# A recurrent attention with a gated feed-forward: the state update moved into the chunk's product, and all chunks ordered anew

## The chip, the cores and the metric

The kernel runs on one core of a Trainium2 chip. The metric is the device time of one execution in microseconds (us), as the median of several runs. The engines are TensorE (PE in the rows; PEld is its loading of weights), VectorE (DVE), ScalarE (ACT), GpSimd (POOL) and SyncE (SP, which issues the DMAs).

## What is computed

```python
# q, k, v, alpha: (4, 8, 768, 48); w_in: (384, 2048); w_out: (2048, 384)
for t in range(S):
    state = alpha[:, :, t, :, None] * state + np.einsum('bhd,bhe->bhde', k[:, :, t], v[:, :, t])
    y[:, :, t] = np.einsum('bhd,bhde->bhe', q[:, :, t], state)
x = np.ascontiguousarray(attn_out.transpose(0, 2, 1, 3)).reshape(B * S, H * D)   # (3072, 384)
h = x @ w_in
sp = np.where(h > 20.0, h, np.log1p(np.exp(np.minimum(h, 20.0))))
return ((h * np.tanh(sp)) @ w_out).astype(np.float32)
```

## The kernel before

**Chunks.** The 768 steps of each of 4 batches are cut into 6 chunks of 128; the 24 chunks are numbered with the batch running fastest, so chunk n follows chunk n - 4 of the same batch. For each chunk `attention(n)` records these tasks. VectorE makes decays by two scans and multiplies keys and queries with them (L523 to L550). *Scores*: TensorE multiplies keys with queries into two PSUM banks (L570, 16 matmuls, which the trace shows as 32 records, two passes of float32 each). VectorE masks them into `probs` (L580). *Product*: into two further banks, three groups of 8 matmuls: state times queries (only from the second chunk of a batch on), values times the diagonal-free half of `probs` on 128 rows, values times the diagonal blocks on 64 rows (all L625; 16 records a group). A tiny memset on GpSimd between the first and the last group keeps matmuls of different row groups apart. ScalarE and VectorE split the product into a high and a low part (L641, L646; for the first 8 chunks TensorE subtracts, L653, and ScalarE copies, L661), and six small DMAs move rows together.

**State.** For all but the last chunk of a batch there are four steps more: *turn*, 4 transposes of the decayed keys on TensorE into a fifth bank (L732); a copy of them to SBUF on ScalarE (L736, one buffer, tag `kb`); *update*, 8 matmuls of keys with values into a sixth bank (L743); and *gather*, on VectorE, which adds that bank to the decayed state (L753; for the first chunk of a batch a copy on ScalarE, L751).

**Units.** A feed-forward unit takes 2 or 4 chunks and one of 16 slices of 128 hidden columns: 9 matmuls of "up" (L782), a chain of five ScalarE and three VectorE passes (L791 to L817), then three matmuls of "down" for each chunk (L845) into an accumulating bank `o0` to `o3`. There are 106 units.

**What sets the order.** Nothing is issued in the order of recording. `Plan.order` walks all tasks with a planner's cost and latency (table `COST`) and a due time (`key`, shifted by hand in the table `SHIFT`), picks at each step the task that can begin first, and thereby fixes the order of every engine's queue. Each queue runs in order on the chip. PSUM banks come from queues too: two called `att`, two `h`, and `o0` to `o3`; `EARLY_BANKS` lets some chunks use free `h` and `o` banks. Until planned time 130 the planner puts a *fill* matmul (L895, whose result nobody reads) wherever it sees TensorE with nothing to do. The framework adds the semaphores; two engines that touch one PSUM bank are kept apart by a semaphore, whatever columns they touch.

Of the kernel before, what the change touches and what calls it, by code (L numbers as in the profile page):

```python
# [27 lines left out]
B, H, S, D = 4, 8, 768, 48  # L28
DM, FF = 384, 2048
P = 128  # L30
C = 128
HALF = C // 2
NCH = S // C
NPAIR = H // 2
R = 112
# [32 lines left out]
    0: "h att o2 att o2 o0".split(),  # L68
    1: "att att att att h att".split(),
    2: "att o1 o1 o3 att att".split(),  # L70
    3: "att h o3 o1 att o0".split(),
    4: "att att att h att att".split(),
    5: "o3 att att o2 att att".split(),
    6: "att att att att h att".split(),
    7: "att att att att o2 o3".split(),
# [3 lines left out]
        4: -2, 5: -2, 7: 2.79, 21: -1,  # L79
    },  # L80
    "unit": {
# [3 lines left out]
    },  # L85
    "weight": {
        0: -5, 4: 5.7, 11: 4, 14: 2, 15: 1,
    },
    "weight check": {
        5: 15, 9: 5,  # L90
    },
}
X_PE = 8
W_PE = 3
# [16 lines left out]
class Task:  # L111
    def __init__(self, engine, cost, late, key, emit, port):
        self.engine, self.cost, self.late, self.key, self.emit = engine, cost, late, key, emit
        self.port = port
        self.needs, self.behind, self.uses, self.begin = [], [], [], None


class Plan:
# [14 lines left out]
    def add(self, engine, cost, late, key, emit, needs=(), uses=(), behind=(), port=False):  # L133
        t = Task(engine, cost, late, key, emit, port)
        t.needs, t.uses, t.behind = list(needs), list(uses), list(behind)
        for u in t.uses:
            u.left += 1
            u.key = min(u.key, key)
        self.tasks.append(t)
        return t  # L140

    def order(self):
# [9 lines left out]
        moving, landed = 0.0, []  # L152
# [40 lines left out]
        while len(done) < n + fills:  # L193
            best = None
            for e in ENGINES:
                first = None
                for t in waiting[e][:WINDOW]:
# [3 lines left out]
                    r = max(r, free[e], port_free if t.port else 0.0)  # L201
# [22 lines left out]
            free[e] = at + t.cost  # L224
            if e == "SP":
# [19 lines left out]
WINDOW = 150  # L245
QUEUE = 8
# [7 lines left out]
    "scan": (1.16, 1.27), "inverse": (0.09, 0.21), "mult": (0.6, 0.72), "half mult": (0.345, 0.46), "check": (0.2, 0.34),  # L254
    "state": (0.365, 0.4), "state0": (0.31, 0.35), "mask": (0.49, 0.63),
    "scores": (1.02, 1.05), "y0": (1.1, 1.2), "y": (1.77, 1.79), "turn": (0.42, 0.64),
    "turned": (0.43, 0.57), "update": (0.7, 0.9),
    "x hi": (0.275, 0.415), "x lo": (0.34, 0.455),
    "down": (0.531, 0.8), "stash": (0.4, 0.53), "join": (0.47, 0.59), "result": (0.5, 0.7),
}  # L260
for _n in range(1, 5):
    _c = 128 * _n
    COST["up", _n] = (9 * (0.4333e-3 * _c + 0.009), 9 * (0.4333e-3 * _c + 0.009) + 0.205)
    COST["exp", _n] = (0.22 + 0.836e-3 * _c, 0.29 + 0.836e-3 * _c)
# [7 lines left out]
def fast_path(ctx, tc, qka, v, w, out, good):  # L272
# [203 lines left out]
    def attention(n):  # L476
# [5 lines left out]
        banks = EARLY_BANKS.get(n, ["att"] * 6)  # L482
# [103 lines left out]
        def product():  # L586
            p = [by_slot(within(z)) for z in y_buf]
            ops = []

            def head(j, a, lead, l, r, t=slice(0, C)):  # L590
                m, side = j // 2, 1 ^ a ^ (j // 2)
                wide = D if side else HALF
                ops.append(
                    (
                        p[m][64 * side : 64 * side + wide, j % 2, t], l(wide), r,
                        j % 2 == 0 and lead,
                    )
                )

            if not first:  # L600
                for i in range(2):
                    for j in (i, i + 2):
                        for a, r in enumerate((0, 64)):
                            head(
                                j, a, True, lambda w: st[r : r + D, j * D : j * D + w],
                                Q()[r : r + D, j],
                            )
            for j in range(NPAIR):
                for a in (1, 0) if j < 2 else (0, 1):
# [4 lines left out]
                    )  # L614
            for i in range(2):
                for j in (i, i + 2):
                    rows = slice(HALF * (j // 2), HALF * (j // 2) + HALF)
                    for a in (1, 0) if j < 2 else (0, 1):
                        h = (2 * j + a) * D
                        head(  # L620
                            j, a, False, lambda w: V()[rows, h : h + w],
                            probs[slot[a]][rows, i, 0], slice(0, HALF),
                        )
            for m, (o, l, r, begins) in enumerate(ops):
                made = nc.tensor.matmul(  # L625
                    o, l, r, start=begins, stop=m >= len(ops) - 2, skip_group_check=True
                )
                if not first and m == 7:
                    apart = nc.gpsimd.memset(between, 0.0)
                    tc.add_manual_dep(apart.ins, made.ins.name, SYNCED, reason="rows apart")  # L630
                if not first and m == 16:
                    tc.add_manual_dep(made.ins, apart.ins.name, SYNCED, reason="rows apart")
# [56 lines left out]
        if not first:  # L689
# [6 lines left out]
        t_sc = add("PE", *COST["scores"], key + 0.2, scores, [*t_k, t_q], [q_buf, *sc_buf])  # L696
# [6 lines left out]
        ]  # L703
        t_y = add(
            "PE", *COST["y0" if first else "y"], key + 0.5, product,
            [*t_mask, t_q, got_v, *t_decay], [q_buf, v_buf, *y_buf],
# [20 lines left out]
        kb_buf, u_buf, ks_buf = bank(banks[4]), bank(banks[5]), plan.buffer("kb")  # L727

        def turn():
            p = by_pair(within(kb_buf))  # L730
            for j in range(NPAIR):
                nc.tensor.transpose(p[:, j, :R], K()[:, j], ident[:R, :R])  # L732

        def turned():
            t = new(ks_buf, [P, NPAIR, R], f"ks{n}")
            nc.scalar.copy(t, by_pair(kb_buf.tile)[:, :, :R])  # L736

        def update():
            p = by_pair(within(u_buf))
            for j in range(NPAIR):  # L740
                for a, wide in ((0, HALF), (1, D)):
# [427 lines left out]
```

## Time and profile before

| | us |
|---|---|
| three runs | 516.72, 517.62, 518.61 |
| median | 517.62 |
| the profiled execution's own time | 516.63 |
| its span in the trace | 514.9 |
| TensorE busy | 506.9 |
| ScalarE busy | 393.6 |
| VectorE busy | 377.4 |

The span lies 1.7 us below the execution's own time: what lies around it isn't traced. The records of matmuls overlap, since they are pipelined, so a group's own "us" in a timeline is longer than the time to the next group's start. The time that a group costs is read from start to next start.

### The profile page before, as it was taken

To read this page: it belongs to the slowest core of one execution; us is meant where nothing else is said; L and a number is where in the kernel's file an instruction comes from. 1 tells how busy PE (TensorE), PEld (TensorE's weight loads), DVE (VectorE), ACT (ScalarE), POOL (GpSimd) and SP (SyncE) were. 2 spreads that over 40 slices of the span, in tenths; PEclk is the share of its full clock that TensorE was granted. 3 is DMA by queue.
4 is the path that set the end of the run, shared out by engine and by line. 5 is a ranking of instruction groups with operands and counts; after the bars stand their busy time and mean duration, and the time that the engine had idled before them with its cause. 6 is when DMAs were issued, how large, how long until landed. Compare 5 with 4: busy or idle time off the path is not lost.

```text
span 514.9 us, 11417 instructions
## 1 busy us (share of the span) xinstructions
PE 506.9 (98%) x4448; PEld 439.7 (85%) x4448; DVE 377.4 (73%) x729; ACT 393.6 (76%) x908; POOL 4.6 (1%) x34
## 2 busy tenths in 40 slices
PE   7999999999999999999999999999999999999996
PEld 4688899898988888888889888889878899999996
DVE  8999999999987878677765567676479544444442
ACT  2587789988699989988977676668766767787774
POOL 2000000000000000000000000000000000000000
PEclk9999999999999999999999999999999999999999
DMA  7684425332336765356420042220032000010001
GB/s 275 232 281 160 149 92 201 122 123 64 122 125 209 238 238 206 125 208 210 147 84 0 1 148 86 87 84 1 16 133 86 9 9 0 23 40 1 0 2 65
DMA packets 20074, 56.68 MB, mean 110 GB/s; under 512 B 4016, under 2 KB 12464, under 8 KB 20016
## 3 DMA queue, kind: packets, MB, share of 16 engines
q1 hardware_dynamic: 20016, 55.91, 31.3%
q8 instruction: 36, 0.59, 0.4%
q14 instruction: 22, 0.18, 0.1%
HBM read 48.82 MB, written 4.72 MB: 104 GB/s over the span
## 4 chain that ended last, share of the span: by engine, by line
PE 94%; DVE 3%; DMA 1%; ACT 0%; issue 0%; DVEq 0%
PE bank L845 40%; PE bank L782 39%; PE bank L625 6%; PE bank L570 3%; PE bank L743 2%; PE bank L732 1%; PE bank L895 1%; DMA qka<-in_qka_dram 1%; DVE probs L580 1%; DVE rest L523 0%; DVE qka L540 0%; PE bank L653 0%; DVE w_lead L397 0%; PE bank L431 0%; DVE qka L550 0%
## 5 line engine op out<-in xcount | busy, mean ns | idle before, releaser
L845 PE MATMUL bank<-wo,g 128*128 128x384 f32 x1152 | 224.2, 341 | 0.0
L782 PE MATMUL bank<-xs,wi 128*128 128x512 f32 (+1 forms) x954 | 217.0, 374 | 0.0
L845 PEld LDWEIGHTS bank<-wo,g 128*128 128x128 f32 x1152 | 198.7, 188 | 7.1 <-ACT state L751 0.2
L782 PEld LDWEIGHTS bank<-xs,wi 128*128 128x128 f32 x954 | 166.6, 188 | 28.5 <-DVE y L801 0.2
L817 DVE TENSOR_TENSOR g<-t,g 128x512 fp32r<-128x512 f32 (+1 forms) x106 | 67.0, 636 | 50.3 <-ACT g L814 50.2
L801 DVE SCALAR_TENSOR_TENSOR y<-u,bank 128x512 f32<-128x512 f32 (+1 forms) x106 | 66.8, 631 | 42.0 <-ACT u L791 41.3
L791 ACT ACTIVATE u<-bank 128x512 f32<-128x512 f32 (+1 forms) x106 | 58.5, 552 | 45.0 <-PE bank L782 44.5
L814 ACT ACTIVATE g<-t 128x512 fp32r<-128x512 f32 (+1 forms) x106 | 61.3, 584 | 22.1 <-PE bank L845 16.1
L810 DVE SCALAR_TENSOR_TENSOR t<-y,t 128x512 f32<-128x512 f32 (+1 forms) x106 | 67.0, 632 | 14.8 <-ACT t L807 14.5
L804 ACT ACTIVATE t<-t,tenth 128x512 f32<-128x512 f32 (+1 forms) x106 | 72.1, 681 | 2.1
L797 ACT ACTIVATE t<-u 128x512 f32<-128x512 f32 (+1 forms) x106 | 62.5, 590 | 10.1 <-DVE g L817 8.6
L807 ACT ACTIVATE t<-t 128x512 f32<-128x512 f32 (+1 forms) x106 | 61.9, 584 | 0.7
L523 DVE TENSOR_TENSOR_SCAN rest<-qka,behind 112x516 f32<-112x516 f32 x24 | 29.4, 1226 | 4.6 <-DMA qka<-in_qka_dram 4.4
L540 DVE TENSOR_TENSOR_SCAN qka<-qka,ahead 112x516 f32<-112x516 f32 x24 | 29.3, 1223 | 0.0
L580 DVE COPY_PREDICATED probs<-causal,bank 128x384 f32<-128x384 uint32 x48 | 25.7, 583 | 2.5 <-PE bank L570 2.5
L625 PEld LDWEIGHTS bank<-probs,v 128*64 128x64 f32 (+3 forms) x768 | 20.7, 128 | 6.4 <-issue 3.3
L641 ACT ACTIVATE xs<-bank 112x256 fp32r<-112x256 f32 x48 | 16.1, 376 | 13.1 <-PE bank L625 12.8
L625 PE MATMUL bank<-probs,v 128*64 128x64 f32 (+3 forms) x768 | 25.6, 227 | 0.3
L570 PEld LDWEIGHTS bank<-qka 48*64 48x64 f32 x768 | 18.0, 133 | 6.5 <-issue 4.1
L570 PE MATMUL bank<-qka 48*64 48x64 f32 (+1 forms) x768 | 21.6, 250 | 0.4 <-issue 0.4
L791 ACT ACTIVATION_READ_ACCUMULATOR u<-bank 128x1 f32 x106 | 20.7, 195 | 0.0
L535 DVE TENSOR_TENSOR qka<-qka,rest 112x256 f32<-112x256 f32 x48 | 19.2, 401 | 0.0
(79 smaller groups left out, 321.2 us busy)
## 6 DMA issues: line engine op xcount, KB each, us to landing
qka<-in_qka_dram SPq DMA_DIRECT2D x22, 770.5 KB, 4.6
ws<-in_wp_dram SPq DMA_DIRECT2D x16, 768.0 KB, 4.3
wc<-in_wp_dram SPq DMA_DIRECT2D x16, 768.0 KB, 5.1
v<-in_vp_dram SPq DMA_DIRECT2D x24, 192.0 KB, 4.4
out_dram<-osb SPq DMA_DIRECT2D x16, 192.0 KB, 2.2
xs<-xs SPq DMA_DIRECT2D x144, 16.0 KB, 2.3
out_dram<-part SPq DMA_DIRECT2D x8, 192.0 KB, 2.8
qka<-in_qka_dram SPq DMA_DIRECT2D x2, 258.5 KB, 3.5
```

The lines of the kernel that those rows point to most:

```text
L570: nc.tensor.matmul(p[a][to, i, blocks], K()[r : r + D, j, to], q.rearrange("p (x t) -> p x t", t=HALF), start=True, stop=True,)
L625: made = nc.tensor.matmul(o, l, r, start=begins, stop=m >= len(ops) - 2, skip_group_check=True)
L782: nc.tensor.matmul(p[:, :N], wi[:, z, s, fs], x[:, s, :, a], start=m == 0, stop=m == len(passes) - 1,)
L791: nc.scalar.activation(wide(u), wide(h), AF.Exp, scale=-1.0, accum_out=uchk[:, at : at + 1])
L797: nc.scalar.activation(wide(t), wide(u), AF.Square, bias=1.0, scale=2.0)
L801: nc.vector.scalar_tensor_tensor(wide(y), wide(u), 0.5, wide(h), ALU.add, ALU.mult)
L804: nc.scalar.activation(wide(t), wide(t), AF.Ln, bias=tenth, scale=0.1)
L807: nc.scalar.activation(wide(t), wide(t), AF.Exp, scale=-1.0)
L810: nc.vector.scalar_tensor_tensor(wide(t), wide(y), 0.4, wide(t), ALU.mult, ALU.mult)
L814: nc.scalar.activation(g.tile[:, 0, :N], wide(t), AF.Copy)
L817: late[mybir.EngineType.DVE] = nc.vector.tensor_tensor(g.tile[:, 1, :N], wide(t), g.tile[:, 0, :N].bitcast(F32), ALU.subtract)
L845: made = nc.tensor.matmul(o.tile[:, :DM], g.tile[:, a, j * C : (j + 1) * C], wo[:, z, f], start=begins and m == 0, stop=end and m == 2,)
```

## The change

The 8 matmuls of the update are issued within the product: behind the second group (128 rows) and ahead of the third (64 rows). Their sums go to columns 256 to 447 of the product's first bank, which the product leaves free; the sixth bank is gone, and a chunk takes 5 banks. The turn and ScalarE's copy of the keys are now due right after the keys are decayed (0.15 and 0.2 behind the chunk's key instead of 0.8 and 0.85), and the product waits for that copy. The gather reads the product's first bank, which ScalarE (high part), and VectorE or TensorE (low part), read or write as well. The last chunk of a batch has no update, as before.

The planner takes 0.2 us off a task when two of scores and products follow each other on TensorE, many of its task times are new, and the tables `EARLY_BANKS` (19 chunks instead of 8) and `SHIFT` are new throughout, so all queues have a new order.

```diff
 SHIFT = {
     "chunk": {
-        4: -2, 5: -2, 7: 2.79, 21: -1,
+        5: -0.9, 6: -1.5, 7: -0.06, 10: 1, 11: 1, 12: -4, 13: -2, 14: -0.5, 15: 2.3, 17: -1,
...
-                    r = max(r, free[e], port_free if t.port else 0.0)
+                    saved = SAME if e == "PE" and small and t.small[0] else 0.0
+                    r = max(r, free[e] - saved, port_free if t.port else 0.0)
...
-        banks = EARLY_BANKS.get(n, ["att"] * 6)
+        banks = EARLY_BANKS.get(n, ["att"] * 5)
...
         def product():
             p = [by_slot(within(z)) for z in y_buf]
+            change = within(y_buf[0])[:, 2 * C : 2 * C + NPAIR * D].rearrange(
+                "p (j e) -> p j e", j=NPAIR
+            )
...
+            if not last:
+                for j in range(NPAIR):
+                    for a, wide in ((0, HALF), (1, D)):
+                        h = (2 * j + a) * D
+                        nc.tensor.matmul(
+                            change[64 * a : 64 * a + wide, j],
+                            ks_buf.tile[:, j, 64 * a : 64 * a + wide],
+                            V()[:, h : h + D], start=False, stop=True, skip_group_check=True,
+                        )
...
+            t_kb = add("PE", *COST["turn"], key + TURN_AT, turn, t_k, [q_buf, kb_buf])
+            t_ks = add("ACT", *COST["turned"], key + TURN_AT + 0.05, turned, [t_kb], [kb_buf, ks_buf])
         t_y = add(
-            "PE", *COST["y0" if first else "y"], key + 0.5, product,
-            [*t_mask, t_q, got_v, *t_decay], [q_buf, v_buf, *y_buf],
+            "PE", *COST["y0" if first else "y last" if last else "y"], key + 0.5, product,
+            [*t_mask, t_q, got_v, *t_decay] + ([] if last else [t_ks]),
+            [q_buf, v_buf, *y_buf] + ([] if last else [ks_buf]), small=(not first, True),
         )
...
-        kb_buf, u_buf, ks_buf = bank(banks[4]), bank(banks[5]), plan.buffer("kb")
...
-        def update():
-            p = by_pair(within(u_buf))
-            for j in range(NPAIR):
-                for a, wide in ((0, HALF), (1, D)):
-                    h = (2 * j + a) * D
-                    nc.tensor.matmul(
-                        p[64 * a : 64 * a + wide, j, :D], ks_buf.tile[:, j, 64 * a : 64 * a + wide],
-                        V()[:, h : h + D], start=True, stop=True,
-                    )
...
         def gather():
-            u = by_pair(u_buf.tile)[:R, :, :D]
+            u = y_buf[0].tile[:R, 2 * C : 2 * C + NPAIR * D].rearrange("p (j e) -> p j e", j=NPAIR)
...
-        t_u = add("PE", *COST["update"], key + 0.9, update, [t_ks, got_v], [ks_buf, v_buf, u_buf])
         done_state[b] = [
             add(
-                *(("ACT", *COST["state0"]) if first else ("DVE", *COST["state"])), key + 1.0,
-                gather, [t_u, t_y, *t_decay], [u_buf],
+                *(("ACT", *COST["state0"]) if first else ("DVE", *COST["state"])), key + 0.7,
+                gather, [t_y], [y_buf[0]],
             )
         ]
```

What that makes of the queues is seen at two places. The first is TensorE's queue behind the product of chunk 16 (`probs` and `v16` are the product's operands, `ks16` the turned keys, `wi` belongs to "up", `wo` to "down"). Before, with the turn and the update between unit work:

```order
L625 MATMUL bank_3873<-probs0_93,v16_3429 64x64
L625 MATMUL bank_3873<-probs1_95,v16_3429 48x64
L782 MATMUL bank_3904<-xs1_112,wi_109 128x512 x9
L732 MATMUL bank_3920<-ident_69,qka16_3420 128x112 x4
L845 MATMUL bank_2961<-wo_110,g57_3853 128x384 x3
L845 MATMUL bank_2968<-wo_110,g57_3853 128x384 x3
L743 MATMUL bank_3939<-v16_3429,ks16_3929 64x48
L743 MATMUL bank_3939<-v16_3429,ks16_3929 48x48
```

And now, from the end of the update to the scores of chunk 17:

```order
L644 MATMUL bank_3863<-v16_3285,ks16_3809 64x48
L644 MATMUL bank_3863<-v16_3285,ks16_3809 48x48
L617 MATMUL bank_3863<-probs1_95,v16_3285 64x64
L617 MATMUL bank_3863<-probs0_93,v16_3285 48x64
L617 MATMUL bank_3864<-probs0_93,v16_3285 64x64
L617 MATMUL bank_3864<-probs1_95,v16_3285 48x64
...
L592 MATMUL bank_3907<-qka17_3604 64x128
L592 MATMUL bank_3908<-qka17_3604 64x128
```

The update no longer stands between two groups of unit work: it stands inside the product, and here the next chunk's scores follow the product directly.

The second place is the shared bank of chunk 4, on TensorE's queue (L653 before, L683 now: the subtraction that makes the low part), with what each row waits for. Before:

```order
L653 MATMUL bank_670<-xs1_112,minus_ident_82 112x256 [waits Activation_49]
L653 MATMUL bank_671<-xs1_112,minus_ident_82 112x256 [waits Activation_49]
L743 MATMUL bank_733<-v4_456,ks4_726 64x48 [waits Activation_49]
L743 MATMUL bank_733<-v4_456,ks4_726 48x48
L743 MATMUL bank_733<-v4_456,ks4_726 64x48
```

And now:

```order
L617 MATMUL bank_680<-probs0_93,v4_467 64x64
L617 MATMUL bank_680<-probs1_95,v4_467 48x64
L867 MATMUL bank_727<-wo_110,g0_625 128x384 x3
L683 MATMUL bank_122<-xs1_112,minus_ident_82 112x256 [waits DVE_49]
L867 MATMUL bank_671<-wo_110,g1_716 128x384 x3
L683 MATMUL bank_680<-xs1_112,minus_ident_82 112x256 [waits Activation_49]
```

The first subtraction now stands behind VectorE's gather, which reads the same bank, `bank_122`.

## Rows read from the trace of the kernel before

**Rows 1.** The page: span, TensorE's busy share, and the chain that ended last.

```profile
span 514.9 us, 11417 instructions
...
PE 506.9 (98%) x4448; PEld 439.7 (85%) x4448; DVE 377.4 (73%) x729; ACT 393.6 (76%) x908; POOL 4.6 (1%) x34
...
PEclk9999999999999999999999999999999999999999
...
PE 94%; DVE 3%; DMA 1%; ACT 0%; issue 0%; DVEq 0%
```

**Rows 2.** Waits of PE, whole span: line, releaser, us in total, times, longest.

```profile
PE bank L895 <- DVE behind L311: 2.6, 1, 2.6
PE pf L958 <- DVE every L944: 1.0, 1, 1.0
PE bank L570 <- issue: 0.4, 1, 0.4
```

**Rows 3.** PE timeline, 247 to 259 us: start, us, line, operands, count of records.

```profile
247.22 1.31 PE L845 MATMUL bank<-wo,g 128*128 128x384 f32 x6
248.45 0.90 PE L570 MATMUL bank<-qka 48*64 48x128 f32 x32
249.28 2.35 PE L782 MATMUL bank<-xs,wi 128*128 128x512 f32 x9
251.57 0.66 PE L625 MATMUL bank<-qka,state 48*48 48x128 f32 x16
252.16 1.06 PE L625 MATMUL bank<-probs,v 128*64 128x64 f32 x32
253.16 2.88 PE L845 MATMUL bank<-wo,g 128*128 128x384 f32 x15
...
257.93 0.67 PE L743 MATMUL bank<-v,ks 128*64 128x48 f32 x16
258.53 4.37 PE L782 MATMUL bank<-xs,wi 128*128 128x512 f32 x18
```

**Rows 4.** PE timeline, 95 to 97 us: large groups alone.

```profile
95.50 1.21 PE L845 MATMUL bank<-wo,g 128*128 128x384 f32 x6
96.54 2.24 PE L782 MATMUL bank<-xs,wi 128*128 128x512 f32 x9
```

**Rows 5.** PE timeline, 25 to 32 us: an update beside a product, and a product alone.

```profile
25.12 0.61 PE L743 MATMUL bank<-v,ks 128*64 128x48 f32 x15
...
25.61 1.05 PE L625 MATMUL bank<-probs,v 128*48 128x64 f32 x31
26.59 1.33 PE L782 MATMUL bank<-xs,wi 128*128 128x256 f32 x9
...
30.70 1.04 PE L625 MATMUL bank<-probs,v 128*64 128x64 f32 x32
31.67 0.67 PE L743 MATMUL bank<-v,ks 128*64 128x48 f32 x16
```

**Rows 6.** PE timeline, 2 to 24 us: the fill matmuls (L895) and the scores (L570).

```profile
2.58 5.54 PE L895 MATMUL bank<-behind 112*128 112x384 bf16 x18 [2.58 <-DVE behind L311]
8.06 0.90 PE L570 MATMUL bank<-qka 48*64 48x128 f32 x32
...
18.09 0.50 PE L895 MATMUL bank<-behind 112*128 112x384 bf16 x2
...
20.21 2.29 PE L895 MATMUL bank<-behind 112*128 112x384 bf16 x13
22.92 0.90 PE L570 MATMUL bank<-qka 48*64 48x128 f32 x32 [0.43 <-issue]
```

**Rows 7.** Busy time by stretch: stretch, its us, then PE, PEld, DVE, ACT.

```profile
20.00:30.00 10.00, 9.57 (x161) 7.47 (x158) 10.00 (x21) 5.45 (x17) 0.00 (x0) 1.00 0.88 324
...
110.00:120.00 10.00, 10.00 (x51) 8.92 (x50) 10.00 (x21) 8.72 (x20) 0.00 (x0) 1.00 0.24 80
200.00:250.00 50.00, 50.00 (x521) 42.55 (x520) 37.03 (x69) 44.37 (x103) 0.26 (x3) 1.00 0.51 180
```

**Rows 8.** The update (L743) by its source line: what its engine waited for.

```profile
  ACT ks L736: 1.4, 5
```

**Rows 9.** VectorE's and ScalarE's groups by line: count, busy us, mean ns, idle before.

```profile
L810 DVE SCALAR_TENSOR_TENSOR t<-y,t 128x512 f32<-128x512 f32 (+1 forms) x106 | 67.0, 632 | 14.8 <-ACT t L807 14.5
...
L753 DVE TENSOR_TENSOR state<-bank,state 112x192 f32<-112x192 f32 x16 | 5.6, 353 | 9.8 <-PE bank L743 9.8
```

**Rows 10.** ScalarE's groups by line, in the same columns.

```profile
L641 ACT ACTIVATE xs<-bank 112x256 fp32r<-112x256 f32 x48 | 16.1, 376 | 13.1 <-PE bank L625 12.8
...
L736 ACT COPY ks<-bank 128x448 f32<-128x448 f32 x20 | 10.6, 530 | 3.4 <-PE bank L732 3.4
```

More of the change, by code (lines that the diff above doesn't have):

```diff
@@ L93 @@
 X_PE = 8
+TURN_AT = 0.15
 W_PE = 3
@@ L131, in buffer, with add @@
         return made
-    def add(self, engine, cost, late, key, emit, needs=(), uses=(), behind=(), port=False):
+    def add(
+        self, engine, cost, late, key, emit, needs=(), uses=(), behind=(), port=False,
+        small=(False, False),
+    ):
         t = Task(engine, cost, late, key, emit, port)
+        t.small = small
         t.needs, t.uses, t.behind = list(needs), list(uses), list(behind)
@@ L151, in order @@
         done, n, port_free = [], len(self.tasks), 0.0
-        moving, landed = 0.0, []
+        moving, landed, small = 0.0, [], False
         def ready(t):
@@ L245 @@
 WINDOW = 150
+SAME = 0.2
 QUEUE = 8
@@ L253 @@
     "w check": (0.92, 1.2),
[L254 to L257, printed above, removed]
+    "scan": (1.16, 1.27), "inverse": (0.09, 0.21), "mult": (0.6, 0.72), "half mult": (0.32, 0.46), "check": (0.2, 0.34),
+    "state": (0.275, 0.4), "state0": (0.28, 0.35), "mask": (0.49, 0.63),
+    "scores": (0.93, 1.0), "y0": (1.38, 1.48), "y": (2.05, 2.15), "y last": (1.68, 1.75), "turn": (0.37, 0.6),
+    "turned": (0.43, 0.57), "update": (0.65, 0.87),
     "x hi": (0.275, 0.415), "x lo": (0.34, 0.455),
-    "down": (0.531, 0.8), "stash": (0.4, 0.53), "join": (0.47, 0.59), "result": (0.5, 0.7),
+    "down": (0.521, 0.79), "stash": (0.4, 0.53), "join": (0.47, 0.59), "result": (0.5, 0.7),
 }
@@ L607, in product @@
                             )
+                apart = nc.gpsimd.memset(between, 0.0)
+                tc.add_manual_dep(apart.ins, made.ins.name, SYNCED, reason="rows apart")
             for j in range(NPAIR):
@@ L619, in product @@
                         h = (2 * j + a) * D
-                        head(
+                        made = head(
                             j, a, False, lambda w: V()[rows, h : h + w],
-                            probs[slot[a]][rows, i, 0], slice(0, HALF),
+                            probs[slot[a]][rows, i, 0], slice(0, HALF), stop=i == 1,
                         )
[L624 to L632, printed above, removed]
+                        if apart:
+                            tc.add_manual_dep(
+                                made.ins, apart.ins.name, SYNCED, reason="rows apart"
+                            )
+                            apart = None
         tile_at, place = X_AT[n]
@@ L703, in attention, with turn, turned @@
         ]
+        if not last:
+            kb_buf, ks_buf = bank(banks[4]), plan.buffer("kb")
+            def turn():
+                p = by_pair(within(kb_buf))
+                for j in range(NPAIR):
+                    nc.tensor.transpose(p[:, j, :R], K()[:, j], ident[:R, :R])
+            def turned():
+                t = new(ks_buf, [P, NPAIR, R], f"ks{n}")
+                nc.scalar.copy(t, by_pair(kb_buf.tile)[:, :, :R])
+            t_kb = add("PE", *COST["turn"], key + TURN_AT, turn, t_k, [q_buf, kb_buf])
+            t_ks = add("ACT", *COST["turned"], key + TURN_AT + 0.05, turned, [t_kb], [kb_buf, ks_buf])
         t_y = add(
-            "PE", *COST["y0" if first else "y"], key + 0.5, product,
-            [*t_mask, t_q, got_v, *t_decay], [q_buf, v_buf, *y_buf],
+            "PE", *COST["y0" if first else "y last" if last else "y"], key + 0.5, product,
+            [*t_mask, t_q, got_v, *t_decay] + ([] if last else [t_ks]),
+            [q_buf, v_buf, *y_buf] + ([] if last else [ks_buf]), small=(not first, True),
         )
```

63 lines of the change are left out of this document (33 added, 30 removed), and 7 rows, old and new, of the table SHIFT.

## The prediction

> **What bounds the kernel now.** I read the page's shares first, then who TensorE waits for, then TensorE's timeline, and last the busy time by stretch. TensorE is busy for 506.9 of 514.9 us, the chain that ended last runs through it for 94%, and its clock is granted in full throughout [rows 1]. Busy alone proves little for pipelined matmuls, but TensorE's whole list of waits has three entries: 2.6 us before its first fill, 0.4 us before the scores at 22.92, 1.0 us at the very end [rows 2]. From the first scores at 8.06 us [rows 6] on it is therefore a stream without holes, and the time is the sum of what stands in its queue. The question is what the change takes out of that queue, and whether new holes appear.
>
> Two prices follow from the timeline. **A run of small matmuls costs more than itself.** Six "down" matmuls between two large groups take 1.04 us (95.50 to 96.54) [rows 4]; six that follow an update and precede scores take 1.23 (247.22 to 248.45) [rows 3]. So going into a run of scores, product or update and coming out of it costs 0.19 us together. **An update** by itself takes 0.60 us from start to next start (257.93 to 258.53) [rows 3].
>
> **The change part by part.** *The update inside the product.* The trace has one place where it stood so already, by chance: one update directly ahead of another chunk's values part. The two take 1.47 us (25.12 to 26.59) [rows 5]; the values part alone takes 0.97 (30.70 to 31.67) [rows 5] to 1.00 (252.16 to 253.16) [rows 3], so the update costs 0.47 to 0.50 there, 0.485 in the middle, and saves 0.115 of its 0.60. One of the 20 updates has this already: 19 x 0.115 = **-2.2 us**. Bounds from the nearest rows: at the pace of the scores (0.83 us for 32 records [rows 3]) its 16 records would cost 0.42; at that of the state group (251.57 to 252.16, 0.59 for 16 [rows 3]), or if the array had to be set anew for it, 0.59 to 0.60. That is -3.4 to -0.2. I take 0.485, since it is the same instructions beside the same neighbour.
>
> *Fewer runs.* I counted in both orders the runs of scores, products and updates that large matmuls, turns or fills enclose: 65 before, 42 now. 17 of the 23 are updates that stood alone; the other 6 are scores that now follow a product directly (five times) or other scores (once). 23 x 0.19 = **-4.4 us**; a hundredth either way in the price is 0.2.
>
> *More fills.* The queue holds 60 fill matmuls instead of 50. 14 instead of 18 precede the first scores; those only cover a wait, because the scores begin when VectorE has made chunk 0's decays, and its queue is unchanged up to there, so they are worth nothing. Behind the first scores there are 46 instead of 32. Between a group of 2 (0.50 us) and one of 13 (2.29 us) lie 11 fills, so one costs 0.163 [rows 6]: 14 x 0.163 = **+2.3 us**. This is where the early gain goes: VectorE is busy for 10.00 of 10.00 us between 20 and 30 us and still between 110 and 120 [rows 7], its work per chunk is the same as before, and a TensorE that is done sooner waits for it. Eight chunks' worth of the saving is about what the added fills cost.
>
> *The turn moved ahead.* 20 turns before and now; they leave the place behind the product for one near the scores. The place is free for TensorE. What it adds is a wait: the product cannot begin its update before ScalarE has copied the turned keys, 0.530 us each [rows 10]. Before, 5 of the 20 updates had to wait for that copy, 1.4 us in all [rows 8], though only on the weight side and with unit work in front. In the new order I laid the row durations end to end along TensorE's queue: from a turn's last transpose to its product at least 2.2 us pass on every chunk, 2.9 or less on six of them, and the update stands some 1 us further back in the product. A copy of 0.53 us fits with one ScalarE pass ahead of it. I cost it at nothing; without that cover it is a rival below.
>
> *DMA and the rest.* The loads of chunk 2 now stand ahead of the row-moving DMAs on SP's queue, which can only bring them earlier. The "rows apart" memset keeps its place, with the update added between its two ends. A bank less per chunk frees PSUM, and the product's first bank is held until the gather. Walking VectorE's early queue with the row durations, the masks of chunk 4 end at about 40 us in both orders, so the early stage gains nothing and loses nothing. From an "up" to its first "down" at least 5.6 us pass in the new order (5.4 before, without a hole). All of this I cost at nothing, within 0.5 us either way.
>
> **Sum:** -2.2 - 4.4 + 2.3 = -4.3 us. The profiled execution took 516.63 us, 1.7 more than its span, and would take 512.3. It lies 1.0 below the median of the runs shown, 517.62, so as a median I expect 513.3 us.
>
> **The rivals.** *A. The shared bank brings holes.* Before, the gather read a bank of its own and waited for TensorE alone [rows 9]. Now it shares one with the splitting of the product, and the new order has waits that weren't there: ScalarE's high part waits for the gather on 10 chunks, the gather for ScalarE on 4, and TensorE's subtraction for the gather on chunks 4 and 6. Each hands on 0.353 us of gather [rows 9] or 0.376 of copy [rows 10], and up to one VectorE pass of 0.632 that stands ahead [rows 9], so 0.35 to 1.0 us. On TensorE's own queue that is two chunks, 0.7 to 2.0 us; the others fall on ScalarE, which is busy for 44.4 of 50 us in the middle [rows 7], and some reach TensorE late. I price the rival at +2 us: 515.3. The Trainium skill (PSUM — Partial Sum Buffer, "PSUM bank collisions raise a hardware error") says that no two engines may touch the same bank and partition quadrant at once, reads against reads included; by that rule gather and splitting must run one after the other even though their columns differ. No run so far shows a collision; the rows of the order show the waits, and the rule would make them unavoidable for this layout.
>
> *B. The product waits for ScalarE (slower).* The mechanism is the turn's copy arriving late. Before it was off TensorE's path, now every one of 20 products depends on it, and ScalarE's queue runs in order: three passes of a unit ahead of the copy, with 0.53 for itself, make more than 2.2 us. It decides at 4.3 / 20 = 0.22 us per product, where the gain is gone, and is a loss beyond the measurement's reach from 0.3. At 0.4 us a product it costs 8 us: 521.3. For it: ScalarE is the second busiest engine in that stage. Against it: the distances above, and that before only 5 copies came last, by 0.28 us each.
>
> *C. The update doesn't join the product's rhythm.* If writing other columns of the bank, or keys instead of `probs` as operand, needs the same setting-up as a group of its own, the 0.60 stays and only the runs are saved: -0.2 - 4.4 + 2.3 = -2.3, 515.3. The chance neighbours [rows 5] speak against it.
>
> *D. More gain.* At the pace of the scores, and with the 0.4 us hole before chunk 2's scores gone: -3.4 - 4.8 (0.21 a run) + 2.3 - 0.4 = -6.3: 511.3.
>
> **How the numbers follow.** Forecast, between 511.8 and 514.6: 0.58. A or C, 514.6 to 516.1: 0.17. D, below 511.8: 0.10. A and C together, or half of B, so that nothing is left: 0.09. B in full: 0.06. A difference under 0.3% (1.55 us) can't be told from none here. So faster 0.85, same 0.09, slower 0.06. The range from 511.0 to 516.2 takes in the forecast, A, C and most of D.
>
> **What would show each step right or wrong.** The matmuls of the update should follow the second product group without a gap and take 0.45 to 0.50 us in all; about 0.60 means C. A product with its update should run for about 2.07 us from start to next start in place of 1.59 and 0.60 (251.57 to 253.16 and the update's own [rows 3]). TensorE's list of waits should still have nothing of weight after the first scores; an entry for the product waiting for the turned keys' copy means B, one for the subtraction waiting for the state means A. The fills should total 60, with scores of chunk 0 at about 8.06 us again and the product of chunk 4 at about 40 us: much later would mean that VectorE's early stage lost time. The granted clock should stay full; if it fell, every price here would be wrong.

## The result, and the profile after

The changed kernel takes **511.22 us** (median of 4 runs, 510.73 to 511.43) where the kernel before takes 517.63 (516.72 to 518.61): a ratio of 0.9874, with a 95% interval of 0.9855 to 0.9894. It is faster by 6.4 us in the medians and by 5.3 in the profiled executions (516.63 and 511.30). The forecast was 513.3 from a sum of -4.3 us: right in its sign and within its range, too small in its size.

The page of the changed kernel, to be laid beside [rows 1]:

```profile
span 509.6 us, 11432 instructions
...
PE 500.6 (98%) x4458; PEld 439.2 (86%) x4458; DVE 377.8 (74%) x729; ACT 390.1 (77%) x908; POOL 4.6 (1%) x34
...
PEclk9999999999999999999999999999999999999999
...
PE 90%; DVE 4%; DMA 2%; ACT 1%; issue 1%; POOL 1%; DVEq 0%; ACTq 0%; POOLq 0%
```

TensorE's busy time fell by 6.3 us, the span by 5.3; the clock is full as before. The chain of waits still runs through TensorE, though for 90% and not 94%: a little more of it now passes over to the other engines. What they make TensorE wait for is in its list of waits (line, releaser, us in total, times, longest), beside [rows 2]:

```profile
PE bank L917 <- DVE behind L333: 2.6, 1, 2.6
PE pf L980 <- DVE every L966: 1.0, 1, 1.0
PE bank L592 <- DVE part L894: 0.5, 1, 0.5
PE bank L740 <- DVE qka L557: 0.5, 1, 0.5
PE bank L592 <- DVE qka L572: 0.2, 1, 0.2
```

The first two are those of before. The two for `qka` lie ahead of or at the first scores; the other, 0.5 us, stands at 204.75 us, where scores wait for VectorE's sum of an output. So TensorE is a stream almost without holes again. From the start of the first scores to the start of the last matmul (the *stream* below) it runs for 503.06 us before (8.06 to 511.12) and for 498.01 after (7.76 to 505.76).

TensorE's timeline after (start, us, line, operands, count of records), at the first scores, in chunk 4, at chunk 7's scores, in chunk 8, and where scores follow a product directly:

```profile
7.76 0.90 PE L592 MATMUL bank<-qka 48*64 48x128 f32 x32 [0.19 <-DVE qka L572]
...
40.47 0.66 PE L617 MATMUL bank<-qka,state 48*48 48x128 f32 x16
...
43.45 0.37 PE L683 MATMUL bank<-xs,minus_ident 112*112 112x256 f32 x1
...
66.20 0.90 PE L592 MATMUL bank<-qka 48*64 48x128 f32 x32
...
134.48 0.66 PE L617 MATMUL bank<-qka,state 48*48 48x128 f32 x16
135.07 0.68 PE L617 MATMUL bank<-probs,v 128*64 128x64 f32 x16
135.56 0.64 PE L644 MATMUL bank<-v,ks 128*48 128x48 f32 x16
136.13 0.46 PE L617 MATMUL bank<-probs,v 64*64 64x64 f32 x16
136.52 3.92 PE L867 MATMUL bank<-wo,g 128*128 128x384 f32 x21
...
290.29 0.46 PE L617 MATMUL bank<-probs,v 64*64 64x64 f32 x16
290.56 0.86 PE L592 MATMUL bank<-qka 48*64 48x64 f32 x32
```

Chunk 8's product with its update (L644) takes 134.48 to 136.52, 2.04 us; a product alone took 1.59 and an update by itself 0.60 [rows 3]. The third group costs 0.39 ahead of a large matmul (136.13 to 136.52), and 0.27 where scores follow (290.29 to 290.56).

The early stage gained nothing. The scores of chunk 7, the last of the first eight, begin at 66.20 us; before, they began here:

```profile
65.46 0.90 PE L570 MATMUL bank<-qka 48*64 48x128 f32 x32
```

By 60 us, 103 large matmuls (up and down) have begun in place of 108. So the whole gain lies behind. VectorE's busy time by stretch, beside [rows 7] (stretch, its us, then PE, PEld, DVE, ACT), shows why one might expect that: VectorE is still busy for nearly all of the early stage.

```profile
20.00:30.00 10.00, 9.88 (x145) 6.59 (x143) 9.89 (x21) 6.69 (x20) 0.00 (x0) 1.00 0.91 334
...
110.00:120.00 10.00, 10.00 (x51) 8.97 (x50) 10.00 (x19) 8.24 (x17) 0.00 (x0) 1.00 0.27 89
```

### The profile page after: what moved, and what is told of

It is laid out like the page before. It is cut to its first block, busy times and chain, and to the rows that moved or that the text cites. A ratio compares the mean times of both kernels' runs of the same rounds, so it can differ in the third digit from the quotient of the medians.

```text
span 509.6 us, 11432 instructions
## 1 busy us (share of the span) xinstructions
PE 500.6 (98%) x4458; PEld 439.2 (86%) x4458; DVE 377.8 (74%) x729; ACT 390.1 (77%) x908; POOL 4.6 (1%) x34
## 4 chain that ended last, share of the span: by engine, by line
PE 90%; DVE 4%; DMA 2%; ACT 1%; issue 1%; POOL 1%; DVEq 0%; ACTq 0%; POOLq 0%
PE bank L804 38%; PE bank L867 37%; PE bank L617 7%; PE bank L592 3%; PE bank L644 2%; DMA qka<-in_qka_dram 2%; PE bank L740 1%; DVE rest L545 1%; DMA ws<-in_wp_dram 1%; PE bank L917 1%; DVE probs L602 1%; PE bank L453 0%; DVE qka L562 0%; PE bank L683 0%; DVE qka L572 0%
## 5 line engine op out<-in xcount | busy, mean ns | idle before, releaser
L867 PE MATMUL bank<-wo,g 128*128 128x384 f32 x1152 | 219.7, 339 | 0.0
L617 PE MATMUL bank<-probs,v 128*64 128x64 f32 (+3 forms) x768 | 26.9, 227 | 0.2
L592 PE MATMUL bank<-qka 48*64 48x128 f32 (+1 forms) x768 | 21.2, 248 | 0.7 <-DVE part L894 0.5
```

The lines of the kernel that those rows point to most:

```text
L592: nc.tensor.matmul(p[a][to, i, blocks], K()[r : r + D, j, to], q.rearrange("p (x t) -> p x t", t=HALF), start=True, stop=True,)
L617: return nc.tensor.matmul(p[m][64 * side : 64 * side + wide, j % 2, t], l(wide), r, start=j % 2 == 0 and lead, stop=stop, skip_group_check ...
L867: made = nc.tensor.matmul(o.tile[:, :DM], g.tile[:, a, j * C : (j + 1) * C], wo[:, z, f], start=begins and m == 0, stop=end and m == 2,)
```

## Experiments

Three groups of kernels ran beside the kernel before: first the kernel before itself with three versions of the change, then the changed kernel with three more, last four on prices and on the early stage. The kernel before had a median of 517.33, 517.52 and 516.90 us in the three.

### Both kernels once more

The kernel before, unchanged:

> The kernel before, once more. Its profiled execution (516.63 us) lay 1.0 below the median of its runs (517.62), that of the changed kernel (511.30) did not (511.22), so the traces differ by 5.3 us and the medians by 6.4. Theory A: the runs of before differ among themselves because a hole of TensorE before the scores of chunk 2 (0.43 us in the first trace) grows when the load of chunk 2 lands late; then a second trace shows an hole there of another size (0.4 to 2 us) and the execution's time moves by as much. Theory B: the spread is outside the kernel's stream (in front of the first instruction or behind the last): then the stream from the first scores to the last matmul is 503.05 us again, within 0.1, and the span alone tells nothing of it. Times: 516.7 to 518.6.

Measured: 517.13 us (516.38 to 518.31, 12 runs), ratio 0.9997 [0.9984, 1.001]. The profiled execution took 516.89, with a stream of 503.32 us (7.95 to 511.27). The 0.4 us hole before the third chunk's scores was gone from the list of waits, and the time was none the less the same. That hole is therefore not the reason for the spread. Theory B's test fails too: the stream is not 503.05 within 0.1 but 0.26 us longer, and the execution is longer by as much (516.89 against 516.63). What makes the spread stays open.

The changed kernel, unchanged:

> The changed kernel once more, as the ground for the others on this chip. Its first look took 511.2 us (median) and 511.30 in profile, with a stream of 498.0 us from the first scores to the last matmul. If the extra microsecond by which the medians differ more than the profiles (6.4 against 5.3) belongs to the kernel, this gives 511.2 +- 0.5 again and a ratio of 0.987 to 0.989; if it was chance of the few runs, the ratio comes out near 511.3 / 516.9 = 0.989 to 0.991.

Measured: 510.95 us (510.70 to 511.31, 4 runs), ratio 0.9866 [0.9849, 0.9882]; profiled 511.31, stream 497.88. The larger gain of the medians came again. The profiled executions of the kernel before (516.63 and 516.89) lie below its medians, those of the changed kernel (511.30 and 511.31) do not.

### The update behind the third group

The update's loop was moved from between the second and third group to the end of the product; the rest is the changed kernel.

```diff
-            if not last:
-                for j in range(NPAIR):
-                    for a, wide in ((0, HALF), (1, D)):
...
             for i in range(2):
                 for j in (i, i + 2):
                     rows = slice(HALF * (j // 2), HALF * (j // 2) + HALF)
...
+            if not last:
+                for j in range(NPAIR):
+                    for a, wide in ((0, HALF), (1, D)):
```

> The changed kernel with the update's 8 matmuls behind the product's third group instead of ahead of it; queues otherwise the same. My theory (the place in the product saves the setting-up of the array for another row grouping, about 0.15 us each): the update now stands behind 64-row matmuls and has to change back to 128 rows, 20 x 0.15 = 3.0 us more than the changed kernel, 514.2. Rival (only the number of matmuls and of runs of small matmuls counts): 511.2.

Measured: 513.70 us (513.59 to 514.22), ratio 0.9927 [0.9902, 0.9951]; its stream took 500.79, 2.8 us more than that of the changed kernel, 0.14 for each of 20 chunks: near the theory's 514.2 and far from the rival's 511.2. Chunk 8 in its timeline:

```profile
136.57 1.06 PE L617 MATMUL bank<-probs,v 128*64 128x64 f32 x32
137.57 0.67 PE L658 MATMUL bank<-v,ks 128*64 128x48 f32 x16
138.16 3.91 PE L867 MATMUL bank<-wo,g 128*128 128x384 f32 x21
```

Here the update costs 0.59 us (137.57 to 138.16) and second and third group 1.00, together 1.59; in the changed kernel the same three take 1.45 (135.07 to 136.52). So being in the product isn't enough: **the update must stand beside the group with which it shares its form.** Its rows and the second group's name tiles of 128 rows, the third group's tiles of 64 (`64*64` in the row of the changed kernel); behind the third group the form changes once more, and 0.14 us is what that costs. The trace has the same split in each of the 20 chunks: ahead of the update the second group takes 0.49 us to the next start, ahead of the third group 0.61; the update takes 0.57 in its place inside the product, 0.60 behind the third group.

### The update twice

The update's loop stands twice in each product, one behind the other; the state is then advanced twice by the same change.

> The changed kernel with the update's 16 matmuls issued twice, one set behind the other, in each of the 20 products (the state is then advanced twice by the same change). It prices the update in the product's rhythm by itself. From the changed kernel's timeline (product with update 2.04 us, product without 1.59): 20 x 0.45 = 9.0 us, so 520.0 to 520.5. By the 0.485 of the prediction: 9.7, so 520.8. If what the product saved is only that the array is set up once, and the update's own records run no faster than alone (0.60): 12, so 523. Holes would hide part of it: under 8 us would mean that TensorE waited for something else there all along.

Measured: 520.00 us (519.72 to 520.38), as the first of the three figures had it: +8.8 to +9.1 on the two medians of the changed kernel; stream 506.81, +8.93. Chunk 8:

```profile
138.41 0.66 PE L617 MATMUL bank<-qka,state 48*48 48x128 f32 x16
...
139.50 0.58 PE L644 MATMUL bank<-v,ks 128*48 128x48 f32 x15
...
140.92 3.92 PE L876 MATMUL bank<-wo,g 128*128 128x384 f32 x21
```

The product takes 2.51 us (138.41 to 140.92) instead of 2.04: 0.47 for the second update, 0.45 in the mean of all 20. So an update in this place costs 0.45 to 0.47, and it shows in full in the time: nothing else held TensorE.

### Structure, task times and tables apart

Three kernels hold the changed product and turn. The first has the old shifts, early banks and task times, the second the new tables with the old task times, the third the new task times with the old tables. The edit, in the planner's numbers:

```diff
-    "scores": (0.93, 1.0), "y0": (1.38, 1.48), "y": (2.05, 2.15), "y last": (1.68, 1.75), "turn": (0.37, 0.6),
+    "scores": (1.02, 1.05), "y0": (1.56, 1.66), "y": (2.23, 2.25), "y last": (1.77, 1.79), "turn": (0.42, 0.64),
...
-SAME = 0.2
+SAME = 0.0
```

(and, for the old tables, `EARLY_BANKS` and `SHIFT` of before, less the sixth bank.) What came of it, with runs of small matmuls and fills behind the first scores counted in each order:

| kernel | us | ratio | runs | late fills |
|---|---|---|---|---|
| old tables, old times | 515.48 | 0.9962 [0.9948, 0.9976] | 48 | 46 |
| new tables, old times | 514.23 | 0.9938 [0.9914, 0.9963] | 45 | 38 |
| old tables, new times | 517.65 | 1.0005 [0.9993, 1.0017] | 48 | 61 |
| both new (the change) | 510.95 | 0.9866 [0.9849, 0.9882] | 42 | 46 |

> The update in the product and the keys turned first, as in the changed kernel, but with the hand-made tables and the task times of the kernel before (a chunk's sixth bank left out, the product's time raised by 0.46 us for the update, nothing off for neighbours). TensorE's queue has 48 runs of small matmuls (before 65, changed 42) and 46 fills behind the first scores, as the changed kernel has. My theory (runs and rhythm pay, the new tables pay only by 6 runs more, 0.19 us each): 512.4. Rival (the gain is in the new order and banks; old tables with the new structure leave TensorE waiting): 514 to 518, with new entries in TensorE's waits.

The rival held. The fold alone brings 1.9 us. TensorE's waits in that kernel (L670 is the subtraction, L579 the scores, L727 the turn):

```profile
PE bank L670 <- DVE state L765: 0.7, 1, 0.7
PE bank L579 <- DVE qka L559: 0.5, 2, 0.4
PE bank L727 <- DVE qka L544: 0.4, 1, 0.4
PE bank L670 <- ACT state L763: 0.4, 1, 0.4
```

The two for `state` are those of rival A: the subtraction stands behind the gather that shares its bank.

> The changed kernel with its new tables of order and banks, but the old task times in the planner: 38 fills behind the first scores instead of 46 and 45 runs of small matmuls instead of 42, so its queue is worth 8 x 0.163 - 3 x 0.19 = 0.7 us less. Theory S (the time is the content of TensorE's queue plus its holes, and the tables are what closes the holes): 510.5 to 512.0, with holes of under 1 us. Rival (the new times do it: the tables fit only the times that they were made with): 513.5 to 516, with waits of 2 us and more on TensorE's list, as in the kernel with both taken back.

The rival held here as well. Its queue has 8 fills fewer, and yet its stream took 500.97 us, 3.0 more than the change: the holes came back.

```profile
PE bank L617 <- DVE probs L602: 1.1, 1, 1.1
PE bank L683 <- ACT state L776: 0.4, 1, 0.4
PE bank L867 <- DVE ahead L550: 0.3, 1, 0.3
```

> The changed kernel with its new task times, but the shifts and early banks of before: 48 runs and 61 fills behind the first scores. Theory S: the planner, told the right times, sees the waits of the early stage and puts fills into them: 15 x 0.163 + 6 x 0.19 = +3.6 us on 511.2, so 514 to 516, with few waits on TensorE's list. Rival (the right times are enough for a good order): 511 to 513. Either way it says what the new tables are worth by themselves.

Theory S has the sign and is too low by 1.7 us: 517.65 (516.77 to 519.12), no gain at all. The planner puts 14 of its 61 late fills between 79 and 84 us, where the changed kernel has 3:

```profile
79.40 0.99 PE L904 MATMUL bank<-behind 112*128 112x384 bf16 x5
80.09 2.38 PE L854 MATMUL bank<-wo,g 128*128 128x384 f32 x12
82.31 1.64 PE L904 MATMUL bank<-behind 112*128 112x384 bf16 x9
```

These two groups cost 0.69 and 1.34 us from start to next start. Its stream is 5.5 us longer than that of the change beside it (503.40 and 497.88); 15 fills at 0.163 and 6 runs at 0.19 make 3.6 of it, and its list of waits behind the start of the first scores has 1.4 us in place of 0.3. On the fold alone, new times bring nothing (a loss of 2.2 us) and new tables 1.3, but both together 4.5: the tables fit only the times with which they were made.

### What the fills are for

All 46 late fills left out, and in the other kernel every second one (`if i >= COLD and i % 2`):

```diff
         def fill():
+            if i >= COLD:
+                return
             nc.tensor.matmul(
```

> The changed kernel without the 46 fill matmuls behind the first scores (the places in all queues stay); they compute nothing that is read. My theory (the fills stand where TensorE would wait for VectorE anyway): the time stays within 0.5 us of 511.2, and TensorE's waits grow by about 2 us. Rival (the fills cost what they take, 46 x 0.163 = 7.5 us, of which the added 14 are 2.3): 504 to 509. If the holes let the clock fall, the granted clock shows it and the time is above 512.

Measured: 513.68 us (513.14 to 517.59), ratio 0.9927 [0.9902, 0.9952]: 2.5 slower than the change. Both prices missed; the clause on the clock held in the profiled execution. By stretch (the number behind POOL's is the granted clock):

```profile
0.00:10.00 10.00, 6.25 (x52) 3.67 (x53) 7.78 (x20) 2.42 (x4) 2.80 (x14) 1.00 0.81 275
10.00:20.00 10.00, 8.36 (x104) 5.03 (x106) 8.65 (x18) 4.54 (x12) 0.00 (x0) 0.73 0.58 219
20.00:30.00 10.00, 9.11 (x92) 6.34 (x90) 6.56 (x14) 3.82 (x11) 0.00 (x0) 0.50 0.73 251
30.00:40.00 10.00, 8.97 (x151) 6.89 (x147) 9.76 (x19) 5.86 (x19) 0.00 (x0) 0.92 0.36 108
```

Between 20 and 30 us the clock is at its lower level, 1.2 instead of 2.4 GHz. Ahead of the fall TensorE had waited 1.17 us for VectorE's mask of the first chunk:

```profile
9.95 0.68 PE L617 MATMUL bank<-probs,v 128*64 128x64 f32 x16 [1.17 <-DVE probs L602]
```

Only this execution was traced, and it is the slowest of the five (517.59 us). Its mean granted clock is 0.981; that of the other four is 0.993 to 0.998, and that of the kernels with fills 0.997 to 1.000 (once 0.994). So none of the four had a fall as long as this one, and yet they took 513.14 to 514.25 us. What makes them 2 us and more slower than the change is not shown.

> The changed kernel with every second of its 46 late fills left out (23 of 0.163 us, 3.7 us of TensorE's work). Theory F (the late fills stand where TensorE would have waited for VectorE anyhow, and their other use is to keep the clock up): 511.2 +- 0.6, the 3.7 us come back as waits, clock full. Rival 1 (a fill is a cost while the clock holds): 507.5 to 509, no new waits. Rival 2 (the clock falls already with half of them): 512 to 514, and the granted clock falls below full between 10 and 40 us as it did without any.

Measured: 510.44 us (510.38 to 510.67), ratio 0.9859 [0.9842, 0.9875]: close to theory F (0.2 us below its band), far from rival 1. It is 0.5 us below the change on the same chip, the two ranges apart by 0.03, and the fastest of the kernels here that leave nothing out of the computation. Its stream took 497.03, 0.85 less than the change beside it. 23 fills of 0.163 are 3.7 us. TensorE's list of waits behind the first scores grew from 0.3 us (the change beside it) to 2.7. Of the 0.85, 0.6 is gained by 82 us and 0.2 where the wait at 204.75 us is gone. The clock stayed full:

```profile
10.00:20.00 10.00, 9.06 (x151) 5.96 (x151) 9.90 (x22) 4.77 (x14) 0.00 (x0) 1.00 0.58 222
20.00:30.00 10.00, 9.41 (x139) 6.38 (x140) 9.88 (x20) 6.93 (x20) 0.00 (x0) 1.00 0.90 315
30.00:40.00 10.00, 9.37 (x130) 7.96 (x129) 9.95 (x23) 7.71 (x25) 0.00 (x0) 1.00 0.62 217
```

### VectorE's part in the early stage

In chunks 0 to 5 the masked copy covers 48 of 384 columns and the decay of the queries 64 of 512, once with all fills and once with half:

```diff
-                nc.vector.copy_predicated(
-                    probs[slot[a]], causal2,
+                w = 8 if n < 6 else HALF
+                nc.vector.copy_predicated(
+                    probs[slot[a]][:, :, :, :w], causal2[:, :, :, :w],
...
-            nc.vector.tensor_tensor(Q(), Q(), front[:, :, 1:], ALU.mult)
+            w = 16 if n < 6 else C
+            nc.vector.tensor_tensor(
+                Q()[:, :, :w], Q()[:, :, :w], front[:, :, 1 : 1 + w], ALU.mult
+            )
```

> The changed kernel with VectorE's work in chunks 0 to 5 made lighter: the masked copy covers 48 of 384 columns, the decay of the queries 64 of 512 (about 1.4 us of VectorE's time less for each chunk, 8 us in all; the scores of these chunks are then not what the reference wants). All 60 fills stay, and the order on TensorE is the same. Theory V (VectorE's queue sets the pace of the first 60 us, and the fills cover what it leaves open): TensorE's queue is the bound now, so only its holes before 60 us can go: 1.5 to 2.5 us, 508.5 to 509.7. Rival (the weights on the DMA queues and ScalarE's copies of them set the pace): 510.5 to 511.2.

Measured: 510.47 us (510.07 to 511.27), ratio 0.9876 [0.9846, 0.9905]; profiled 510.07, 1.2 below the change, median the same within what can be told. That lies just below the rival's band and above theory V's. VectorE's busy time fell by 6.5 us (377.8 to 371.3), not 8. The list of TensorE's waits is down to the two entries of 2.6 and 1.0 us. Of the three waits for VectorE that are gone, two stood ahead of or at the first scores, which now begin at 7.49 us instead of 7.76 or 7.90. The third stood at 204.75 us, far behind chunk 5, and other kernels here lack it as well, so it can't be put down to the lighter VectorE. The stream of 496.98 us is 0.9 shorter than that of the change's second trace: 0.45 by 31.7 us, 0.42 at that third wait. So the early stage gave 0.7 to 0.9 us in all; theory V's 1.5 to 2.5 was too much.

> The same lighter VectorE in chunks 0 to 5, with every second late fill left out. Theory V: with half of the fills out (3.7 us) 3.1 us of waits stood in their place; if those were VectorE's they go too: 505.5 to 507.5. Rival: the waits that came for the fills are for the weights, so nothing more than with the half of the fills alone: 509.5 to 510.5. In between, 507.5 to 509.5: both have a part. If the clock falls for want of fills, the time is worse and the granted clock shows it.

Measured: 508.73 us (508.51 to 510.42), ratio 0.9846 [0.9813, 0.9879], 1.7 below the half of the fills alone: the case in between. The two ran in different groups, and their ratios differ by only 0.0013, within both intervals, but the traces have the difference: a stream of 495.64 us against 497.03, and first scores at 7.49 against 7.87. The waits that stay show both parts: one is for VectorE's gather (L784), the others for ScalarE's copies of weights (`wo`) and of high parts (`xs`). The three longest behind the first scores:

```profile
PE bank L689 <- DVE state L784: 0.4, 1, 0.4
PE bank L623 <- ACT wo L457: 0.3, 1, 0.3
PE bank L810 <- ACT xs L697: 0.3, 1, 0.3
```

### The turn late again

```diff
-TURN_AT = 0.15
+TURN_AT = 0.45
```

> The changed kernel with the turn of the keys due late again, just ahead of the product (due time 0.45 in place of 0.15 behind the chunk's start). The order is made anew from that: 42 runs and 45 late fills, its queue by row prices 0.8 us longer. Theory T (the early turn keeps ScalarE's copy away from the product; late, the product would wait for it as rival B has it): 514 to 518, with entries for the product waiting for ks on TensorE's list. Rival (the planner finds other work to stand between, the turn's place is worth nothing): 511.2 to 512.8, no such entry.

Measured: 511.42 us (511.08 to 511.81), ratio 0.9889 [0.9861, 0.9917]. The rival held: the same time, and TensorE's list of waits has only the two entries of 2.6 and 1.0 us. The planner knows that the product needs the copy and finds work to stand between: the copy ends 0.3 us or more ahead of its update here, 1.8 or more in the changed kernel.

## Why the prediction was right, and where its sizes were off

*A stream without holes; the time is what stands in its queue*: right, before and after. The second update, which adds 8.93 us to the stream and 8.8 to 9.1 to the time, is the plainest proof.

*The update in the product*: the mechanism was right, the size too small. 0.485 was taken for it; 2.04 - 1.59 = 0.45 came, 0.45 to 0.47 in the kernel that has it twice. The saving is 0.15 and not 0.115, 19 x 0.15 = -2.8 us and not -2.2. The 0.485 was the middle of two readings. The 0.50 took for comparison a product with an update behind it (30.70 to 31.67), the 0.47 one with a large group behind it, as here; the second was only 0.02 off. The test "0.45 to 0.50, no gap" came out at its lower end. The Trainium skill (TensorEngine Tiling (Array Packing), "Key Properties") states that changing the tiling mode, and not just the tile, drains TensorE, and under "Available Configurations" it lists 128 rows by 64 columns and 64 by 64 as modes of their own. The prices in the runs fit that, with 0.12 to 0.14 us a change: second group and update are of the one form, third group and scores of the other, and between groups of one form that cost doesn't show (0.27 for the third group ahead of scores). That a drain is what the time goes to, no row shows. The prediction priced by neighbours without asking for their modes, and so missed the 0.6 of the next point.

*Fewer runs of small matmuls*: 23 x 0.19 = -4.4. The price stands up in the records. A step from one down matmul to the next takes 0.173 us from start to start, from a down to scores or product 0.268; the first down behind a small group takes 0.281: 0.095 and 0.108 more. Added up over the stream, up and down matmuls take 3.43 us less than before, though two new holes of 0.47 and 0.31 stand among them; without these it is 4.2, or 0.18 a run. One thing was missed. On five chunks scores follow a product directly, and there the product's last group costs 0.27 instead of 0.39: -0.6 us more. No experiment priced a run alone; the count and these sums are what stand behind it.

*More fills*: +2.3, and the fills behind the first scores take 6.82 us before and 9.11 after (start to next start), +2.29. What the term means is another matter. Read as a cost of fills it is wrong: half of them gone gives 0.85 us of 3.7, and 0.2 of that is the wait at 204.75 us. Read as the prediction put it, an early stage that gains nothing since TensorE waits for others, it is right: chunk 7's scores begin no earlier (66.20 and 65.46). But "others" isn't VectorE alone. VectorE lighter by 6.5 us, with half of the fills, gives 2.2 to 2.5 us against the change; what TensorE waits for then is mostly ScalarE.

*The turn, the copy, rival B*: costed at nothing, and rightly. The update (L644) has no wait of its own anywhere in the trace after, and a late turn doesn't bring one.

*Rival A, the shared bank*: not on TensorE's list after, though the waits exist. The gather's line in the trace after:

```profile
its engine sat idle before it (us, times) until:
  PE bank L617: 4.1, 6
  ACT xs L671: 1.1, 2
who waited for it (us, times):
  ACT xs L671: 2.9, 5
  PEld bank L683: 0.5, 1
```

ScalarE's high part waited for the gather 5 times (10 were possible), the gather for ScalarE twice (4). On TensorE's matmuls there is a delay of 0.31 us ahead of the subtraction at 43.45 (0.5 on its weight load), no more; the price of +2 was too high by far. With the old tables and times the same wait stands on TensorE with 1.1 us. So the order keeps rival A away, not the layout. The rule of the Trainium skill that the prediction cited (PSUM — Partial Sum Buffer, "PSUM bank collisions raise a hardware error") is neither confirmed nor denied: the semaphores let no two engines touch the bank at once in any run here.

*The sum*: by parts, in the profiled executions: -2.8 for the update, -4.4 for the runs, -0.6 for the direct neighbours, +2.3 for the fills, and about +0.4 for new small holes (0.5 at 204.75 us, 0.3 at 43.45, against the 0.4 that went at 22.92) make -5.1; the stream shrank by 5.05. Each kind of matmul added up from start to next start gives the same: product and update together -3.45, up and down -3.43, scores -0.38, fills +2.29, the rest -0.08. The first scores began 0.30 earlier, of which nothing was forecast; the two traces of each kernel differ there by 0.11 and 0.14. That is -5.3 against -4.3.

*The step to a median* failed. The prediction added 1.0 us, since the profiled execution of the kernel before lay that far below its median, and took for granted that the changed kernel's would too. It does not (511.30 and 511.31 against medians of 511.22 and 510.95). So the forecast was 2.1 us too high: 1.0 from this step, 1.0 from the sizes above. The time fell where rival D had put it (511.3), but not by D's parts: the update didn't reach the pace of the scores (0.42). That the two agree is luck. Why the kernel before scatters more widely than the changed one (516.1 to 519.1 against 510.7 to 511.4) stays open; the three kernels with old tables or old times scatter as widely (514.28 to 516.58, 513.80 to 515.89, 516.77 to 519.12).

*What the prediction did not ask*: whether the structure or the new order brings the gain. It counted runs and fills in the new order, so it had both; the fold alone would have been worth 1.9 us.

## What to carry to other kernels

A small group of matmuls on a full TensorE is priced by its neighbours: going in and out costs some 0.2 us, a change between tiles of 128 and 64 rows another 0.12 to 0.14, so put groups of one form side by side, and take a price from a place with the same groups on both sides. A change of structure that alters who waits for whom needs its order made again with the new times, all of it: here the fold alone gave 1.9 us, with new tables 3.3, with new task times 0, and with both 6.4. Filler work in a stage that another engine paces is nearly free. Without any of it the traced execution lost its full clock for a while, with half of it not, and half was the fastest.

## What the runs showed of the hardware

In the traced execution without late fills TensorE's clock stood at 0.50 from about 14.6 to 31.7 us. The longest wait between the first scores and that fall was 1.17 us. With half the fills the clock stayed at 1.00 to the end of the stream.

That execution took 517.59 us, 3.9 above the median of its kind. Its stream took 502.41 us, but from its last matmul to the end of the span 5.6 us passed, where the profiled executions of all other kernels here show 3.8. The difference comes from one instruction behind the last matmul, TensorE's branch past a second path of the kernel that isn't taken here (L1120). Without fills, and with half of them:

```profile
L1120 PEldq COMPARE_BRANCH  x1: 3402/3402/3402, 511.4 to 511.4; - x1
L1120 PEldq COMPARE_BRANCH  x1: 393/393/393, 506.0 to 506.0; - x1
```

It took 3.40 us instead of 0.39, and the end of the span came 1.8 us later for it. So a part of an execution's time can lie behind the stream, where the order of the queues doesn't reach. Whether that is what widens the spread of the kernel before wasn't shown: both of its traces have 3.8 us there.
